# A gated linear attention and mixture-of-experts kernel on one core: one of two chunk masks done by ACT and GpSimd, row sums of two tiles at a time, keys split whole and placed by DMA

## The chip, the cores and the metric

The kernel runs on one core of a Trainium2 chip. The metric is the device time of one execution in microseconds, as the median of some runs. The core has five engines that each run their own instructions in order: PE (TensorE, matrix products, with weight loads shown apart as PEld), DVE (VectorE), ACT (ScalarE), POOL (GpSimd) and SP (SyncE, which here only issues DMAs). They wait for each other through semaphores. PE writes PSUM; POOL does not touch PSUM in this kernel.

## The reference

Two stages. The first is a gated linear attention over 4 batches, 8 heads, 768 positions and a head of 48; the second is a mixture of 4 attention experts on the first one's output, of which each position uses the best 2.

```python
for t in range(S):                                    # B, H, S, D = 4, 8, 768, 48
    state = alpha[:, :, t, :, None] * state + einsum('bhd,bhe->bhde', k[:, :, t], v[:, :, t])
    y[:, :, t] = einsum('bhd,bhde->bhe', q[:, :, t], state)
x = y.transpose(0, 2, 1, 3).reshape(B, S, H * D)      # 4 x 768 x 384
logits = x @ w_gate                                   # 4 experts, top 2, softmax over the two: w
for e in range(E):                                    # Hd = 64
    q, k, v = x @ wq[e], x @ wk[e], x @ wv[e]
    scores = where(causal, -1e9, scale * (q @ k.T))
    a = exp(scores - scores.max(-1)); a /= a.sum(-1) + 1e-09
    out += (weight of e at each position) * (a @ v @ wo[e])
```

## The kernel before

**First stage, by chunks.** The 768 positions of a batch are cut into 6 chunks of 128; there are 24 chunks, `n` = 0 to 23. For each, SP loads the gates (`al`), queries and keys side by side (`qk`) and values (`v`). `prep_r` (lines 172 to 182) makes the running products of the gates from the chunk's end with a DVE scan (L178) and multiplies the keys by them on POOL (L182). `prep_c` (184 to 190) makes those from its start (L188) and multiplies the queries (L190, DVE). `check` (L194, ACT) squares these products for a test of range at the end, in place; it can run only when both multiplications have read them. `gla_a` (196 to 208) forms the 128 x 128 products of keys and queries of 8 heads, `pa[0]` and `pa[1]`, four heads in each PSUM bank, and multiplies each bank by a causal 0/1 mask on DVE into `ms` (L207, one buffer). `gla_t` transposes the keys (`pt`, copied by ACT to `kt`), `gla_u` updates the state (`pu`; L241 on DVE, L242 on POOL), and `gla_y` multiplies `ms` and the state with values and queries into `py`, which is split into a rounded part `xh` (ACT, L268) and a remainder `xl` (DVE, L269).

**Second stage, by units.** Three chunks make a unit of 384 positions, `u` = 0 to 7; `hf` = u % 2 tells the first or second half of a batch. `front(u)` projects queries and keys of two pairs of experts (`proj`, PSUM `pj`, nine matrix products each), the values (`vproj`) and the gate's weights `gw` (`gate`). A projected tile is again split into a rounded part by ACT and a remainder by DVE. For queries this is done whole in `tq` (L405, L406), and four DMAs on SP's queue put the two halves of the partitions where the scores want them (L412). For keys, whose two experts lie in the two halves of the partitions, two ACT copies and two DVE subtractions write straight to `k0` and `k1` (L421 to L424).

`back(u)` goes through 12 tiles (pair, expert `e`, block `i` of 128 positions). `score` (471 to 510) multiplies queries and keys (`sc`; keys up to the diagonal: 128 to 384 columns in a first half, 512 to 768 in a second), takes the negative maximum on DVE (L491, L495), and lets ACT write exp to `a` (L498), whose running sum goes to `sm`. DVE then adds the one or two partial sums and 1e-9 (L503) and takes the reciprocal (L504); in units 1 to 7 POOL scales the row by it and by the gate's weight (L509), and in unit 0 DVE multiplies the two (L506) and ACT scales (L507). `AHEAD` = 4 scores later `transp` transposes `a` on PE (`tr`, L527) and ACT copies it to `at` (L538). When an expert pair is done, `av` multiplies with the values (`yv`), and at the unit's end `outp` forms `po`, `ot` and the output's DMA. `a` has `AB` = 7 buffers, `q` has `QB` = 6, and all PSUM tiles share 8 banks.

**What sets the order.** Up to the end of `rest` in the last lines of the program the instructions stand in the order of the code (`manual_schedule`). After that the streams are mixed by weights: `back(u)`, `front(u+1)` and `half(u+2)`, which is the first stage of the unit after next. A stream's account is raised by the cost of its matrix products and by `HOP` = 100 at each `yield`. The framework's scheduler then orders each engine's instructions by that sequence as priority and by its own estimate of when they are ready, so a small edit can move rows on every engine.

Of the kernel before, what the change touches and what calls it, by code (L numbers as in the profile page):

```python
# [54 lines left out]
def tile_gla_moe(ctx: ExitStack, tc: tile.TileContext, qk_d, al_d, v_d, wqk_d, wv_d, wo_d, nat_d, vn_d, out_d):  # L55
# [140 lines left out]
    def gla_a(n):  # L196
        t = gl["qk", n]
        ms = work.tile([128, 2, 4, C], F32, name="ms", bufs=1)
        gl["ms", n] = ms
        pa = [gp(f"pa{s}") for s in (0, 1)]  # L200
        for p in range(4):
            for s in (0, 1):
                r = 64 * s
                mm(pa[s][:, C * p:C * p + C], t[r:r + D, p, C:2 * C], t[r:r + D, p, 0:C],
                   110, start=True, stop=True, tile_position=(r, 0))
        for s in (0, 1):
            V.tensor_tensor(ms[:, s], pa[s].rearrange("p (a t) -> p a t", t=C),  # L207
                            mask[:, None, :].to_broadcast([128, 4, C]), OP.mult)
# [182 lines left out]
    def proj(u, pair, which):  # L391
        b, hf = divmod(u, 2)
        xh, xl = gl["x", u]
        col = 256 * which + 128 * pair
        cs = slice(col, col + 128)
        pj = gp("pj")
        i = 0
        for kt in range(3):
            for w, x in ((wqk_h, xh), (wqk_h, xl), (wqk_l, xh)):
                mm(pj[:, :W3], w[:, kt, cs], x[:, kt, :], W3 / 2.4, start=(i == 0), stop=(i == 8))  # L400
                i += 1
        if which == 0:
            mo["sm", u, pair] = SM[hf, pair]
            tq = work.tile([128, 2, W3], F32R, name="tq", bufs=1)
            A.activation(tq[:, 0], pj[:, :W3], AF.Copy)  # L405
            V.tensor_tensor(tq[:, 1], pj[:, :W3], tq[:, 0].bitcast(F32), OP.subtract)  # L406
            qs = []
            for e in (0, 1):
                q = work.tile([128, 2, W3], F32R, name="q", bufs=QB)
                src = tq[64 * e:64 * e + 64].bitcast(F32)  # L410
                for h in (0, 1):
                    SY.dma_start(q[64 * h:64 * h + 64].bitcast(F32), src)  # L412
                qs.append((q[:, 0], q[:, 1]))
            mo["q", u, pair] = qs
        else:
            if hf == 0:
# [4 lines left out]
            A.activation(k0[0:64, ts], pj[0:64, :W3], AF.Copy)  # L421
            A.activation(k1[64:128, ts], pj[64:128, :W3], AF.Copy)
            V.tensor_tensor(k0[64:128, ts], pj[0:64, :W3], k0[0:64, ts].bitcast(F32), OP.subtract)
            V.tensor_tensor(k1[0:64, ts], pj[64:128, :W3], k1[64:128, ts].bitcast(F32), OP.subtract)  # L424
# [46 lines left out]
    def score(u, pair, e, i):  # L471
        b, hf = divmod(u, 2)
        qh, ql = mo["q", u, pair][e]
        ks = mo["k", b, pair][e]
        sm = mo["sm", u, pair]
        ts = slice(128 * i, 128 * i + 128)
        n = 128 * (3 * hf + i + 1)
        c1 = 384 if n == 640 else min(n, 512)
# [16 lines left out]
            V.tensor_tensor(nm, mx[:, 0:1], mx[:, 1:2], OP.min)  # L495
        a = work.tile([128, S], F32, name="a", bufs=AB)
        for x, (c0, c1) in enumerate(pieces):
            A.activation(a[:, c0:c1], pss[x][:, :c1 - c0], AF.Exp, bias=nm, accum_out=sm[:, i, e, x:x + 1])  # L498
# [4 lines left out]
        V.tensor_scalar(den, den, 1e-9, sm[:, i, e, 1:2], op0=OP.add, op1=OP.add)  # L503
        V.reciprocal(cf, den)  # L504
        if u == 0:
            V.tensor_tensor(cf, cf, wt, OP.mult)  # L506
            A.activation(a[:, 0:n], a[:, 0:n], AF.Copy, scale=cf)  # L507
        else:
            G.tensor_scalar(a[:, 0:n], a[:, 0:n], cf, wt, op0=OP.mult, op1=OP.mult)  # L509
# [271 lines left out]
```

## Time and profile before

| | us |
|---|---|
| runs shown | 424.32, 419.24 and 1109.5; median 424.32 |
| profiled execution | 423.59, its span 421.9 |
| PE, DVE, ACT, POOL busy | 360.5, 289.0, 226.2, 123.3 |
| mean granted clock of PE | 0.939 |
| DVE in the masks (48) | 30.9 |
| DVE in sums and reciprocals of tiles (96 each) | 19.8 and 15.2 |
| DVE in the remainders of keys (32) | 8.9 and 8.8 |
| POOL in scaling (84) | 66.8 |

A row of the timeline gives start, duration, engine, line, operation, tiles, shapes, count, and in brackets the engine's idle time before it with what ended it. In a row of groups the count is followed by the busy time, the mean in ns, the idle time before, and who ended most of it. The granted clock is that of PE in a stretch, 1.00 being full speed. An engine that is idle costs something only where another one waits for it in the end.

### The profile page before, as it was taken

How to read it: one execution, taken by the hardware profiler on the slowest of the kernel's cores; microseconds unless marked ns; L12 is line 12 of the kernel's file. 1: busy time of each engine (PE TensorE's matmuls, PEld its weight loads, DVE VectorE, ACT ScalarE, POOL GpSimd, SP SyncE). 2: the span in 40 equal slices, each digit the busy share in tenths (PEclk: the TensorE clock that was granted, in tenths of full speed). 3: DMA queues.
4: the chain of work that ended last, by engine and by line, in shares of the span. 5: the costliest groups of instructions: out<-in, count | busy, mean ns of one | idle time of the engine just before them, and what ended most of it. 6: DMA issues, size and time to landing. Idle time of an engine off the chain costs nothing.

```text
span 421.9 us, 10017 instructions
## 1 busy us (share of the span) xinstructions
PE 360.5 (85%) x3758; PEld 294.6 (70%) x3758; DVE 289.0 (69%) x753; ACT 226.2 (54%) x637; POOL 123.3 (29%) x166
## 2 busy tenths in 40 slices
PE   6879676997797994998979869699999999999992
PEld 4659565886385773787848758378878877987772
DVE  5879799999589968177847777428737843578610
ACT  1254237576237745375344863636545766668941
POOL 3142331221214344025301723304402530134410
PEclk9899699699599998899989989799999999999998
DMA  8943596864371534063246223315134003420101
GB/s 231 331 127 89 138 272 175 230 161 122 111 196 51 158 109 123 15 189 93 89 121 197 82 80 113 75 58 151 47 96 111 2 2 77 131 64 13 57 20 47
DMA packets 20106, 48.03 MB, mean 114 GB/s; under 512 B 2704, under 2 KB 7120, under 8 KB 20048
## 3 DMA queue, kind: packets, MB, share of 16 engines
q1 hardware_dynamic: 16336, 42.11, 37.0%
q10 hardware_dynamic: 3712, 5.18, 3.5%
q8 instruction: 32, 0.52, 0.6%
q14 instruction: 26, 0.21, 0.2%
HBM read 29.98 MB, written 4.72 MB: 82 GB/s over the span
## 4 chain that ended last, share of the span: by engine, by line
PE 53%; DVE 19%; ACT 9%; DMA 8%; issue 6%; POOL 3%; SPq 1%; ACTq 0%; DVEq 0%; POOLq 0%
PE yv L72 11%; PE sc L72 7%; PE pj L72 7%; PE po L72 7%; PE py L72 6%; DMA qk<-in_qk_dram 5%; PE tr L527 5%; ACT a L498 4%; PE pv L72 3%; PE pa L72 3%; DVE mx L491 3%; DVE ms L207 2%; DVE al L188 2%; DVE al L178 2%; DVE qk L190 2%
## 5 line engine op out<-in xcount | busy, mean ns | idle before, releaser
L509 POOL TENSOR_SCALAR a<-a,sc,gw 128x512 f32<-128x512 f32 (+5 forms) x84 | 66.8, 800 | 165.4 <-DVE sc L504 69.9
L498 ACT ACTIVATE a<-sc,mx 128x256 f32<-128x256 f32 (+3 forms) x128 | 68.3, 542 | 25.2 <-DVE mx L495 11.1
L491 DVE TENSOR_REDUCE mx<-sc 128x1 f32<-128x256 f32 (+3 forms) x128 | 60.9, 499 | 20.6 <-PE sc L72 20.2
L527 PE MATMUL tr<-ident,a 128*128 128x128 f32 x336 | 55.4, 289 | 21.8 <-POOL a L509 12.2
L72 PE MATMUL sc<-k,q 128*128 128x384 f32 (+3 forms) x256 | 61.1, 348 | 4.1 <-ACT at L538 3.5
L527 PEld LDWEIGHTS tr<-ident,a 128*128 128x128 f32 x336 | 39.5, 147 | 26.9 <-POOL a L509 13.9
L538 ACT ACTIVATE at<-tr 128x512 f32<-128x512 f32 (+3 forms) x124 | 51.4, 462 | 6.7 <-PE tr L527 4.8
L72 PE MATMUL yv<-at,vg 128*64 128x384 f32 (+2 forms) x324 | 51.1, 414 | 3.6 <-ACT at L538 3.2
L182 POOL TENSOR_TENSOR qk<-qk,al 112x512 f32<-112x512 f32 (+1 forms) x26 | 31.8, 1227 | 71.3 <-DVE al L178 25.8
L72 PEld LDWEIGHTS sc<-k,q 128*128 128x128 f32 x256 | 42.1, 194 | 7.6 <-ACT at L538 3.8
L72 PE MATMUL pa<-qk 48*128 48x128 f32 x384 | 30.7, 298 | 16.0 <-issue 7.7
L72 PEld LDWEIGHTS yv<-at,vg 128*64 128x64 f32 x324 | 25.6, 143 | 24.5 <-issue 14.6
L72 PEld LDWEIGHTS pa<-qk 48*128 48x128 f32 x384 | 25.6, 198 | 19.0 <-issue 17.2
L72 PE MATMUL py<-ms,v 128*32 128x128 f32 x768 | 36.5, 283 | 2.7 <-ACT a L498 2.1
L72 PE MATMUL pj<-xh,wqk_h 128*128 128x384 f32 x96 | 36.7, 383 | 2.3 <-ACT xh L268 1.2
L188 DVE TENSOR_TENSOR_SCAN al<-al,d1c 112x516 f32<-112x516 f32 (+1 forms) x26 | 36.2, 1391 | 0.5
L194 ACT ACTIVATE al<-al 112x1032 f32<-112x1032 f32 x23 | 24.5, 1066 | 18.9 <-POOL qk L182 10.1
L72 PE MATMUL pj<-xl,wqk_h 128*128 128x384 f32 x96 | 33.8, 352 | 0.1
L72 PE MATMUL pj<-xh,wqk_l 128*128 128x384 f32 x96 | 33.6, 350 | 0.0
L178 DVE TENSOR_TENSOR_SCAN al<-al,d1r 112x516 f32<-112x516 f32 (+1 forms) x26 | 30.4, 1168 | 4.4 <-DMA al<-in_al_dram 4.1
L207 DVE TENSOR_TENSOR ms<-pa,mask 128x512 f32<-128x512 f32 x48 | 30.9, 686 | 3.3 <-PE pa L72 2.8
L503 DVE TENSOR_SCALAR sm<-sm 128x1 f32<-128x1 f32 x96 | 19.8, 208 | 18.2 <-ACT a L498 17.1
(100 smaller groups left out, 684.4 us busy)
## 6 DMA issues: line engine op xcount, KB each, us to landing
q<-tq SPq DMA_DIRECT2D x64, 192.0 KB, 3.4
al<-in_al_dram SPq DMA_DIRECT2D x21, 451.5 KB, 4.7
qk<-in_qk_dram SPq DMA_DIRECT2D x21, 448.0 KB, 5.2
v<-in_v_dram SPq DMA_DIRECT2D x24, 256.0 KB, 4.6
out_dram<-ot ACTq DMA_DIRECT2D x24, 192.0 KB, 1.9
al<-in_al_dram SPq DMA_DIRECT2D x6, 225.8 KB, 5.4
qk<-in_qk_dram SPq DMA_DIRECT2D x4, 224.0 KB, 6.2
wqk<-in_wqk_dram SPq DMA_DIRECT2D x1, 768.0 KB, 7.4
```

Source lines behind the costliest of these rows:

```text
L72: return PE.matmul(out, lhsT, rhs, **kw)
L178: V.tensor_tensor_scan(r.rearrange("p a w -> p (a w)"), r.rearrange("p a w -> p (a w)"), d1r[0:P, sl].rearrange("p a w -> p (a w)"), 0.0, ...
L182: G.tensor_tensor(t[0:P, sl, C:2 * C], t[0:P, sl, C:2 * C], r[:, :, 0:C], OP.mult)
L188: V.tensor_tensor_scan(c.rearrange("p a w -> p (a w)"), c.rearrange("p a w -> p (a w)"), d1[0:P, sl].rearrange("p a w -> p (a w)"), 0.0, O ...
L194: A.activation(al, al, AF.Square, accum_out=acc[0:P, n:n + 1])
L207: V.tensor_tensor(ms[:, s], pa[s].rearrange("p (a t) -> p a t", t=C), mask[:, None, :].to_broadcast([128, 4, C]), OP.mult)
L491: V.tensor_reduce(mx[:, x:x + 1], pp[:, :w], axis=AX.X, op=OP.max, negate=True)
L498: A.activation(a[:, c0:c1], pss[x][:, :c1 - c0], AF.Exp, bias=nm, accum_out=sm[:, i, e, x:x + 1])
L503: V.tensor_scalar(den, den, 1e-9, sm[:, i, e, 1:2], op0=OP.add, op1=OP.add)
L509: G.tensor_scalar(a[:, 0:n], a[:, 0:n], cf, wt, op0=OP.mult, op1=OP.mult)
L527: PE.transpose(pt[:, 128 * (j - j0):128 * (j - j0) + 128], a[:, 128 * j:128 * j + 128], ident)
L538: A.activation(dst, src, AF.Copy)
```

## The change

There are five edits.

- **Mask.** From chunk 3 on, the second bank `pa[1]` is copied to `ms` by ACT, and POOL sets to zero in place what lies beyond the diagonal (`affine_select` over 128 x 512). The first bank, and both banks of chunks 0 to 2, stay on DVE.
- **Row sums.** `score` ends with exp. A new step `norm` after every second score adds sums and 1e-9 for two tiles in one DVE operation with two inputs in SBUF, takes both reciprocals in one, and issues two POOL scalings. `sm` is laid out as one tile for each half of a batch.
- **Unit 0** is scaled on POOL as the others are.
- **Keys** of units 1 to 7 are split whole, as queries are, into `tk` (one buffer), and four DMAs of 64 partitions on SP's queue put the parts into `k0` and `k1`. Unit 0 keeps the old way.
- **Numbers.** `AHEAD` is 5 instead of 4; `q` has 5 buffers instead of 6.

```diff
-QB = 6
+QB = 5
-AHEAD = 4
+AHEAD = 5
...
         for s in (0, 1):
-            V.tensor_tensor(ms[:, s], pa[s].rearrange("p (a t) -> p a t", t=C),
-                            mask[:, None, :].to_broadcast([128, 4, C]), OP.mult)
+            src = pa[s].rearrange("p (a t) -> p a t", t=C)
+            if s == 0 or n < HALF:
+                V.tensor_tensor(ms[:, s], src, mask[:, None, :].to_broadcast([128, 4, C]), OP.mult)
+            else:
+                A.activation(ms[:, s], src, AF.Copy)
+                G.affine_select(ms[:, s], ms[:, s], [[0, 4], [1, C]], OP.is_ge, 0.0, base=-(C - 1),
+                                channel_multiplier=1)
...
-            A.activation(k0[0:64, ts], pj[0:64, :W3], AF.Copy)
-            A.activation(k1[64:128, ts], pj[64:128, :W3], AF.Copy)
-            V.tensor_tensor(k0[64:128, ts], pj[0:64, :W3], k0[0:64, ts].bitcast(F32), OP.subtract)
-            V.tensor_tensor(k1[0:64, ts], pj[64:128, :W3], k1[64:128, ts].bitcast(F32), OP.subtract)
+            if u == 0:
...
+            else:
+                tk = work.tile([128, 2, W3], F32R, name="tk", bufs=1)
+                A.activation(tk[:, 0], pj[:, :W3], AF.Copy)
+                V.tensor_tensor(tk[:, 1], pj[:, :W3], tk[:, 0].bitcast(F32), OP.subtract)
+                for e, k in enumerate((k0, k1)):
+                    for h in (0, 1):
+                        SY.dma_start(k[64 * h:64 * h + 64, ts].bitcast(F32), tk[64 * e:64 * e + 64, h].bitcast(F32))
...
-            A.activation(a[:, c0:c1], pss[x][:, :c1 - c0], AF.Exp, bias=nm, accum_out=sm[:, i, e, x:x + 1])
-        eg = 2 * pair + e
-        wt = mo["w", u][:, i, eg:eg + 1]
-        den = sm[:, i, e, 0:1]
-        cf = work.tile([128, 1], F32, name="sc", bufs=4)
-        V.tensor_scalar(den, den, 1e-9, sm[:, i, e, 1:2], op0=OP.add, op1=OP.add)
-        V.reciprocal(cf, den)
-        if u == 0:
-            V.tensor_tensor(cf, cf, wt, OP.mult)
-            A.activation(a[:, 0:n], a[:, 0:n], AF.Copy, scale=cf)
-        else:
-            G.tensor_scalar(a[:, 0:n], a[:, 0:n], cf, wt, op0=OP.mult, op1=OP.mult)
+            A.activation(a[:, c0:c1], pss[x][:, :c1 - c0], AF.Exp, bias=nm, accum_out=sm[:, x:x + 1])
         mo["a", u, pair, e, i] = a
+
+    def norm(u, *tiles):
+        hf = u % 2
+        ix = [6 * pair + 3 * e + i for pair, e, i in tiles]
+        sm = SM[hf][:, ix[0]:ix[1] + 1:ix[1] - ix[0]]
+        cf = work.tile([128, 2], F32, name="sc", bufs=4)
+        V.scalar_tensor_tensor(cf, sm[:, :, 0], 1e-9, sm[:, :, 1], op0=OP.add, op1=OP.add)
+        V.reciprocal(cf, cf)
+        for x, (pair, e, i) in enumerate(tiles):
+            a = mo["a", u, pair, e, i]
+            n = 128 * (3 * hf + i + 1)
+            eg = 2 * pair + e
+            G.tensor_scalar(a[:, 0:n], a[:, 0:n], cf[:, x:x + 1], mo["w", u][:, i, eg:eg + 1], op0=OP.mult, op1=OP.mult)
...
                 score(u, *seq[k])
                 yield
+                if k % 2:
+                    norm(u, seq[k - 1], seq[k])
+                    yield
```

What this does to the order of the engines is shown at three places. The line numbers of the changed kernel differ: its masks are L209 (DVE), L211 (ACT) and L212 (POOL), its maxima L503, its sums L518 and L519, its scaling L524, its transposes L541.

On DVE, in unit 0, about where the second to fifth tiles are summed; `sm` holds partial sums, `sc` here the reciprocals. Before:

```order
L491 TENSOR_REDUCE mx<-sc 128x1
L504 RECIPROCAL sc<-sm_113 128x1
L178 SCALAR_TENSOR_TENSOR al<-al,d1r 112x516
L506 TENSOR_TENSOR sc<-sc,gw 128x1
L503 TENSOR_SCALAR sm_113<-sm_113 128x1 x2
L504 RECIPROCAL sc<-sm_113 128x1
L503 TENSOR_SCALAR sm_113<-sm_113 128x1
L506 TENSOR_TENSOR sc<-sc,gw 128x1
L504 RECIPROCAL sc<-sm_113 128x1 x2
L180 RECIPROCAL d1c_82<-al 112x4
L506 TENSOR_TENSOR sc<-sc,gw 128x1 x2
L188 SCALAR_TENSOR_TENSOR al<-al,d1c_82 112x516
```

In the changed kernel:

```order
L503 TENSOR_REDUCE mx<-sc 128x1 x3
L518 SCALAR_TENSOR_TENSOR sc<-sm_113 128x2
L180 RECIPROCAL d1c_82<-al 112x4
L503 TENSOR_REDUCE mx<-sc 128x1
L519 RECIPROCAL sc<-sc 128x2
L188 SCALAR_TENSOR_TENSOR al<-al,d1c_82 112x516
L518 SCALAR_TENSOR_TENSOR sc<-sm_113 128x2
L190 TENSOR_TENSOR qk<-qk,al 112x4x128
```

The eleven small operations ahead of the scan L188 have become one sum and one reciprocal of two tiles; the second pair's sum stands behind the scan.

On PE, at the end of unit 1. Before, this is the end of chunk 11's `py`, with the values of pair 0 (`yv`) in its midst:

```order
L72 MATMUL sc<-cmaskb,identb 128x128
L72 MATMUL yv<-at,vg 64x384
L72 MATMUL py<-ms,v 32x128 x4
L72 MATMUL py<-qk,S_94 32x128 x4
L72 MATMUL py<-ms,v 32x128 x4
L72 MATMUL py<-qk,S_94 32x128
L72 MATMUL yv<-at,vg 64x384 x7
L72 MATMUL yv<-at,vg 64x256 x2
L72 MATMUL yv<-at,vg 64x128 x2
L72 MATMUL py<-qk,S_94 32x128 x3
```

In the changed kernel the same `yv` follows the unit's last score, and the query projection of unit 2's second pair follows it; 24 transposes come after that projection:

```order
L72 MATMUL sc<-k_759,q 128x512 x2
L72 MATMUL sc<-k_759,q 128x256 x2
L72 LDWEIGHTS identb
L72 MATMUL sc<-cmaskb,identb 128x128
L72 MATMUL yv<-at,vg 64x384 x8
L72 MATMUL yv<-at,vg 64x256 x2
L72 MATMUL yv<-at,vg 64x128 x2
L72 MATMUL pj<-xh,wqk_h 128x384
```

So these twelve instructions of `yv` moved from within chunk 11's `py` to behind the last score.

On POOL, from chunk 5's preparation to unit 0's first tiles (`S` is the state). Before:

```order
L182 TENSOR_TENSOR qk<-qk,al 112x4x128 x2
L242 TENSOR_TENSOR S_94<-st,ev 48x4x48 x2
L182 TENSOR_TENSOR qk<-qk,al 112x4x128 x3
L242 TENSOR_TENSOR S_92<-st,ev 48x4x48 x2
L182 TENSOR_TENSOR qk<-qk,al 112x4x128 x2
```

In the changed kernel:

```order
L182 TENSOR_TENSOR qk<-qk,al 112x4x128 x2
L247 TENSOR_TENSOR S_94<-st,ev 48x4x48 x2
L212 AFFINE_SELECT ms<-ms 128x512 x2
L182 TENSOR_TENSOR qk<-qk,al 112x4x128
L524 TENSOR_SCALAR a<-a,sc,gw 128x128
L524 TENSOR_SCALAR a<-a,sc,gw 128x256
L524 TENSOR_SCALAR a<-a,sc,gw 128x384
L524 TENSOR_SCALAR a<-a,sc,gw 128x128
L182 TENSOR_TENSOR qk<-qk,al 112x4x128
L212 AFFINE_SELECT ms<-ms 128x512
```

The selects of chunks 5 and 6 stand ahead of the multiplication of a later chunk's keys, and unit 0's scalings stand between such multiplications.

More of the change, by code (lines that the diff above doesn't have):

```diff
@@ L128, in tile_gla_moe @@
     acc = consts.tile([128, NG], F32)
-    SM = {}
+    SM = []
     for hf in (0, 1):
-        for pair in (0, 1):
-            SM[hf, pair] = consts.tile([128, 3, 2, 2], F32, name=f"sm{hf}{pair}")
-            G.memset(SM[hf, pair], 0.0)
+        t = consts.tile([128, 2 * NE * 3, 2], F32, name=f"sm{hf}")
+        G.memset(t, 0.0)
+        SM.append(t)
     wraw = {}
@@ L402, in proj @@
         if which == 0:
-            mo["sm", u, pair] = SM[hf, pair]
             tq = work.tile([128, 2, W3], F32R, name="tq", bufs=1)
@@ L420, in proj @@
             ts = slice(W3 * hf, W3 * hf + W3)
-            A.activation(k0[0:64, ts], pj[0:64, :W3], AF.Copy)
-            A.activation(k1[64:128, ts], pj[64:128, :W3], AF.Copy)
-            V.tensor_tensor(k0[64:128, ts], pj[0:64, :W3], k0[0:64, ts].bitcast(F32), OP.subtract)
-            V.tensor_tensor(k1[0:64, ts], pj[64:128, :W3], k1[64:128, ts].bitcast(F32), OP.subtract)
+            if u == 0:
+                A.activation(k0[0:64, ts], pj[0:64, :W3], AF.Copy)
+                A.activation(k1[64:128, ts], pj[64:128, :W3], AF.Copy)
+                V.tensor_tensor(k0[64:128, ts], pj[0:64, :W3], k0[0:64, ts].bitcast(F32), OP.subtract)
+                V.tensor_tensor(k1[0:64, ts], pj[64:128, :W3], k1[64:128, ts].bitcast(F32), OP.subtract)
+            else:
[5 more added lines that the diff above has]
+                        SY.dma_start(k[64 * h:64 * h + 64, ts].bitcast(F32), tk[64 * e:64 * e + 64, h].bitcast(F32))
     def vproj(u, i):
@@ L474, in score @@
         ks = mo["k", b, pair][e]
-        sm = mo["sm", u, pair]
+        sm = SM[hf][:, 6 * pair + 3 * e + i]
         ts = slice(128 * i, 128 * i + 128)
```

## Prediction

> **What bounds the kernel now.** I read the page's totals first, then the busy time by stage, then TensorE's (PE's) idle gaps in the timeline, and last the other engines around one such gap.
>
> ```profile
> span 421.9 us, 10017 instructions
> PE 360.5 (85%) x3758; PEld 294.6 (70%) x3758; DVE 289.0 (69%) x753; ACT 226.2 (54%) x637; POOL 123.3 (29%) x166
> PE 53%; DVE 19%; ACT 9%; DMA 8%; issue 6%; POOL 3%; SPq 1%; ACTq 0%; DVEq 0%; POOLq 0%
> ```
>
> PE is the engine with most to do, and it holds about half of the chain that ended last. The change takes nothing off PE, so what it can win lies in the 61 us in which PE is idle (421.9 less 360.5). The stages differ (span, then PE, PEld, DVE, ACT and POOL busy, then PE's granted clock):
>
> ```profile
> 0.00:40.00 40.00, 31.82 (x383) 25.47 (x383) 30.20 (x48) 14.53 (x31) 12.29 (x33) 0.96 0.67 192
> 40.00:110.00 70.00, 52.44 (x662) 44.45 (x661) 65.06 (x149) 36.84 (x103) 16.62 (x18) 0.86 0.73 190
> 110.00:300.00 190.00, 165.60 (x1694) 133.32 (x1694) 127.84 (x330) 101.67 (x291) 62.08 (x71) 0.93 0.37 107
> 300.00:400.00 100.00, 97.23 (x910) 81.11 (x908) 63.23 (x220) 66.47 (x198) 30.12 (x43) 1.00 0.23 61
> ```
>
> From 40 to 110 VectorE (DVE) is busy 65.06 of 70 us and PE has 17.6 us idle: there DVE sets the pace. From 110 to 300 DVE is busy two thirds of the time and PE still loses 24 us. After 300 PE loses 2.8 us in 100 and nothing is to be had. The first 40 us hold no edited instruction that PE waits for. So the gaps between 40 and 300 are what counts; these are the large ones (start, duration, idle time before in brackets and what ended it):
>
> ```profile
> 46.34 2.08 PE L72 MATMUL pa<-qk 48*128 48x128 f32 x16 [3.84 <-issue]
> 57.95 1.16 PE L72 MATMUL pa<-qk 48*128 48x128 f32 x16 [3.07 <-DVE qk L190]
> 74.35 1.02 PE L72 MATMUL pa<-qk 48*128 48x128 f32 x6 [4.02 <-DVE S L239]
> 104.98 0.69 PE L527 MATMUL tr<-ident,a 128*128 128x128 f32 x2 [1.51 <-DVE k L424]
> 109.67 1.54 PE L72 MATMUL yv<-at,vg 128*64 128x384 f32 x2 [1.81 <-ACT at L538]
> 163.30 0.63 PE L527 MATMUL tr<-ident,a 128*128 128x128 f32 x4 [2.69 <-ACT at L538]
> 167.78 1.54 PE L527 MATMUL tr<-ident,a 128*128 128x128 f32 x6 [3.16 <-POOL a L509]
> 213.78 0.47 PE L527 MATMUL tr<-ident,a 128*128 128x128 f32 x1 [3.06 <-POOL a L509]
> 248.26 1.22 PE L72 MATMUL sc<-k,q 128*128 128x512 f32 x2 [3.51 <-ACT at L538]
> 266.79 0.74 PE L527 MATMUL tr<-ident,a 128*128 128x128 f32 x5 [1.31 <-ACT at L538]
> 270.15 1.54 PE L527 MATMUL tr<-ident,a 128*128 128x128 f32 x6 [2.62 <-POOL a L509]
> ```
>
> They sum to 30.6 us and are of two kinds: chunk preparation late on DVE (the three before pa, 10.9 us), and the end of a unit's tiles, when the transposes `tr` have caught up with scaling (the rest). How a unit's end comes about, at unit 1:
>
> ```profile
> 153.68 1.70 SPq L88 DMA_DIRECT2D qk<-in_qk_dram  x2
> 159.08 0.69 DVE L190 TENSOR_TENSOR qk<-qk,al 112x512 f32<-112x512 f32 x1 [1.97 <-DMA qk<-in_qk_dram]
> 159.20 2.76 POOL L182 TENSOR_TENSOR qk<-qk,al 112x512 f32<-112x512 f32 x2 [6.00 <-DMA qk<-in_qk_dram]
> 160.85 1.06 ACT L194 ACTIVATE al<-al 112x1032 f32<-112x1032 f32 x1 [3.64 <-POOL qk L182]
> 165.73 2.00 POOL L509 TENSOR_SCALAR a<-a,sc,gw 128x768 f32<-128x768 f32 x1 [3.78 <-ACT at L538]
> ```
>
> A load goes out only when a chunk's last reader is done (153.68) and is used at 159.08. DVE, POOL and then ACT sit in order behind it, the last tile is scaled only from 165.73, and PE runs out of other work meanwhile.
>
> **The change part by part.** The prices (count, then busy us and mean ns of one):
>
> ```profile
> L503 DVE TENSOR_SCALAR sm<-sm 128x1 f32<-128x1 f32 x96 | 19.8, 208 | 18.2 <-ACT a L498 17.1
> L504 DVE RECIPROCAL sc<-sm 128x1 f32<-128x1 f32 x96 | 15.2, 159 | 4.3
> L506 DVE TENSOR_TENSOR sc<-sc,gw 128x1 f32<-128x1 f32 x12 | 3.7, 319 | 0.1
> L207 DVE TENSOR_TENSOR ms<-pa,mask 128x512 f32<-128x512 f32 x48 | 30.9, 686 | 3.3 <-PE pa L72 2.8
> L424 DVE TENSOR_TENSOR k<-pj,k 64x384 fp32r<-64x384 f32 x16 | 8.9, 559 | 0.3
> L538 ACT ACTIVATE at<-tr 128x512 f32<-128x512 f32 x48 | 28.6, 605 | 4.7 <-PE tr L527 3.0 <-PE yv L72 1.2
> L509 POOL TENSOR_SCALAR a<-a,sc,gw 128x512 f32<-128x512 f32 x16 | 13.6, 851 | 34.2 <-ACT tq L405 29.9 <-DVE sc L504 3.1 <-ACT at L538 1.1
> L116 POOL TENSOR_SCALAR_AFFINE_SELECT mask<-mask 128x128 f32<-128x128 f32 x1 | 0.3, 293 | 0.0
> L507 ACT ACTIVATE a<-a,sc 128x128 f32<-128x128 f32 (+2 forms) x12 | 5.9, 505 | 6.0 <-DVE sc L506 3.3 <-DVE gw L454 1.2 <-DVE d1c L180 1.1
> ```
>
> Masks: for chunks 3 to 23 one of two DVE multiplications goes, 21 x 0.686 = 14.4 us. In its place stand an ACT copy of the same size out of PSUM (0.605 by the `at` copy, 12.7 us in all) and a POOL select of 128x512, which the trace does not show. Its bounds are 0.293 (the select of a quarter of the columns) and 4 x 0.293 = 1.17; I take 0.9, next to the 0.851 of POOL's one-input pass over the same size: 19 us more on POOL. py follows pa closely only at chunks 3 to 5 (one pj or pv and little else between); a copy and a select, 1.5 us, take the place of the 1.3 us of two masks there, and I charge 1 us for POOL's queue. While the select waits for its copy, the next multiply of keys by their products and the next tile's scaling wait behind it on POOL, and PE's transposes for the latter; on ACT a `kt` copy stands behind the new copy. At a unit's end, where that would hurt, the order has other work on PE (below).
>
> Row sums: 96 x (0.208 + 0.159) + 12 x 0.319 = 39 us leave DVE; 48 pairs of a two-input sum and a reciprocal come. A two-input operation on such a sliver is L506, 0.319; with 0.159 that is 48 x 0.478 = 23 us, or 18 us at the price of L503; I take 18 here and charge the rest below, as a cost, so DVE's net is -21. The wait for exp now is for two tiles at once, and what stands behind it on DVE (maxima, scans) waits with it; before, DVE waited 17.1 us on these sums, so I charge nothing more, and at worst 0.2 x 48 = 10 us.
>
> Keys: in units 1 to 7, 14 DVE operations of 0.559 (7.8 us) and 14 ACT copies go. 56 DMAs come, on SP's queue behind the queries':
>
> ```profile
> 164.27 2.40 SPq L412 DMA_DIRECT2D q<-tq  x4
> q<-tq SPq DMA_DIRECT2D x64, 192.0 KB, 3.4
> ```
>
> That is 0.6 us an issue and 3.4 us to landing. A key is projected during the preceding unit's tiles, over 10 us of PE work ahead of its first score, so I take 0; without that cover a unit's start waits 2.4 + 3.4 = 5.8 us. The loads behind them on SP can be 2.4 us later a pair, but most stand waiting for a py anyway. One q buffer fewer makes SP wait for three scores of the running unit; same answer.
>
> Unit 0: 12 ACT passes of 0.505 become POOL passes of at most 0.851. DVE in all: -14.4 - 21 - 7.8 = -43 us; ACT about even; POOL +19 + 8.
>
> Now the gaps, place by place. Preparation (10.9 us): up to 74 us DVE loses four masks (2.7) and the sums of five tiles (3.4), and gets about 1.2 back; the first gap is another matter, as its scan is blocked:
>
> ```profile
> 41.60 3.91 DVE L188 TENSOR_TENSOR_SCAN al<-al,d1c 112x516 f32<-112x516 f32 x1
> 42.62 1.80 POOL L170 TENSOR_TENSOR wo_l<-wo,wo_h 128x768 fp32r<-128x768 f32 x1
> ```
>
> The scan ends 1.1 us after POOL's pass does, at 45.51. I take -4 of 10.9. Unit 0's end (3.3): the other seven tiles' sums and ACT's passes go, -2. Unit 1's end (5.85): five tiles instead of four are outstanding, and the order puts the whole `yv` of pair 0 between the last score and the first of these transposes. Such a `yv`, and a projection with and without a gap before it, take in the chain:
>
> ```profile
> 169.32 2.88 PE pj L72 x9
> 172.21 3.61 PE yv L72 x24
> 179.44 1.63 PE pj L72 x9
> ```
>
> So 3.4 to 3.6 us of work that ran before the wait now runs inside it: -5 of 5.85. Unit 2's end has the shorter `yv`: -2.5 of 3.06. The gap at 248 is ACT and DVE behind a load, and its order is unchanged: -0.5. Unit 3's end (3.93) is like unit 1's: -3. Sum -17. The projection after the gap at 167 took 2.88 instead of 1.63: 1.25 us more go with each gap that closes, -4 for three or four.
>
> Costs: the new two-input sums and the scans meet more POOL work, and L506 took 0.160 more than the one-input L504 beside it: 48 x 0.160 = 7.7 us of DVE, a third of it on the path, +3; masks +1; in the tail two scalings instead of one follow the last exp, +1. So -17 - 4 + 5 = -16 on the profiled execution, which took 423.6 (1.7 around its span; the median of the runs shown is 424.3): **408 us**, and by the bounds of the places 400 to 416.
>
> The Trainium skill, SBUF — State Buffer, section "Who interferes with whom", says that a DVE operation with two SBUF inputs and a POOL operation that reads SBUF exclude each other for the whole instruction. The scan of 3.91 us over POOL's passes agrees. It speaks against this change, which adds both kinds; taken to its end it is the second rival.
>
> **Rivals.** First, the loads bind. Rows 153.68 to 159.20 show every engine behind a transfer that the change does not start sooner. Then only preparation and unit 0's end gain, 6 us, less about 2: 419. Against it: the load's 5.4 us did not change, but PE gets 3.5 us more to do meanwhile.
>
> Second, DVE and POOL exclude each other. From 40 to 110 POOL gets 6 selects and 12 scalings, 6 x 0.9 + 12 x 0.6 = 12.6 us; if all of it holds up scans and sums there, it eats what DVE is freed of: the 6 us of those stages fall away, and I put 2 more on the unit ends: 416. For it: the scan at 41.60. Against it: POOL is busy 16.62 of 70 there, and few scans of that stage are as long.
>
> Third, slower: POOL becomes the last engine at every unit's end. If the last pair is scaled later than PE has `yv` and projection for (5.2 us after the last score), PE waits for a select (0.9) and a second scaling (0.851) more at each of 8 ends, +14; four lost clocks, +5; preparation's -4 stands: 423.6 + 15 = 438. For it: the POOL wait in three of the gaps above, and a buffer of `a` less to spare. Against it: POOL is at 29% of the span.
>
> Fourth, better: all gaps but that at 248 close, -27, with -5 for the clock and the same +5: 397.
>
> **How the numbers follow.** Forecast 0.55, loads 0.18, exclusion 0.10, slower 0.11, better 0.06. The range is 396 to 426, which leaves out the slower case and some ends, under 2 in 10; the forecast's own is 400 to 416. A measurement of this kernel can tell about 2% from no change, so below 415.8 is faster and above 432.8 slower: of the forecast nearly all (0.53), of exclusion and loads little (0.04), and the better case give 0.63 faster; the third rival mostly gives 0.11 slower; 0.26 is left for within 2%.
>
> **What would show it.** Right: DVE busy near 250 us (289 less 43, plus what exclusion gives back), POOL near 150, PE's waits for POOL's `a` at unit 1, 2 and 3's ends under 1 us, and 40 to 110 with PE idle under 13 us in the same work. The first step to fail would be the select: a mean over 1.2 us, or py waiting for it. The pair's sum at a mean over 0.35 shows exclusion. Gaps of 3 us before `tr` with DVE behind L190 show that loads bind. If PE waits for POOL's `a` more than 12 us in all, the third rival holds. The prediction is wrong if PE's idle time stays within 5 us of 61, or falls by over 30.

## The result, and the profile after

| | before | changed |
|---|---|---|
| median of the runs, us | 422.70 | 402.14 |
| ratio, 95% interval | | 0.953 [0.945, 0.961] |
| profiled execution, its span, us | 423.59, 421.9 | 407.95, 406.1 |
| PE busy, PE idle, us | 360.5, 61.4 | 358.7, 47.4 |
| mean granted clock of PE | 0.939 | 0.945 |

The change is faster, by 20.6 us in the medians. The profiled execution of the changed kernel was a disturbed one, some 6 us longer and at a lower clock (0.945) than its other runs (0.952 to 0.958), so its gaps can be read by place, but its span, its PE busy time and its total of idle time compare only roughly with those of the other kernels. The page's totals, as shown of before, are now:

```profile
span 406.1 us, 9981 instructions
PE 358.7 (88%) x3758; PEld 297.7 (73%) x3758; DVE 258.1 (64%) x610; ACT 224.0 (55%) x632; POOL 154.1 (38%) x197
```

DVE lost 31 us of work and POOL got 31. By stage (span, then PE, PEld, DVE, ACT and POOL busy, then PE's granted clock; unit 0 ends near 104 now, near 110 before):

```profile
40.00:104.00 64.00, 50.48 (x702) 43.53 (x701) 57.54 (x116) 33.11 (x92) 37.85 (x37) 0.93 0.81 208
104.00:290.00 186.00, 169.02 (x1763) 139.06 (x1767) 119.43 (x286) 106.84 (x309) 72.19 (x86) 0.94 0.48 130
290.00:384.00 94.00, 93.95 (x848) 79.79 (x842) 50.21 (x159) 64.35 (x192) 30.73 (x44) 1.00 0.34 86
```

In the first stretch PE idles 13.5 us (17.6 before), in the second 17.0 us, where from 110 to 300 it was 24.4. The gaps of PE in its timeline, at the places of the prediction's list and near them (idle time in brackets, and what ended it):

```profile
48.43 1.16 PE L72 MATMUL pa<-qk 48*128 48x128 f32 x16 [2.18 <-POOL wo_l L170]
57.99 2.08 PE L72 MATMUL pa<-qk 48*128 48x128 f32 x16 [4.12 <-DVE qk L190]
73.12 1.16 PE L72 MATMUL pa<-qk 48*128 48x128 f32 x16 [1.11 <-DVE sc L519]
99.43 0.52 PE L541 MATMUL tr<-ident,a 128*128 128x128 f32 x3 [1.35 <-DVE tk L433]
102.50 0.45 PE L541 MATMUL tr<-ident,a 128*128 128x128 f32 x1 [2.55 <-DVE st L246]
104.36 1.31 PE L541 MATMUL tr<-ident,a 128*128 128x128 f32 x5 [1.42 <-DVE xl L274]
159.82 0.74 PE L541 MATMUL tr<-ident,a 128*128 128x128 f32 x5 [0.89 <-DVE yl L573]
201.06 0.44 PE L541 MATMUL tr<-ident,a 128*128 128x128 f32 x2 [0.94 <-POOL a L524]
202.42 0.52 PE L541 MATMUL tr<-ident,a 128*128 128x128 f32 x3 [0.93 <-DVE yl L573]
208.68 0.62 PE L72 MATMUL po<-wo_h,yl 128*128 128x384 f32 x2 [1.61 <-DVE yl L573]
224.22 0.66 PE L541 MATMUL tr<-ident,a 128*128 128x128 f32 x4 [2.21 <-POOL a L524]
237.88 0.73 PE L72 MATMUL sc<-k,q 128*128 128x512 f32 x2 [2.14 <-ACT at L552]
256.21 2.15 PE L541 MATMUL tr<-ident,a 128*128 128x128 f32 x15 [0.50 <-DVE yl L573]
```

The first three are the preparation, 7.4 us in place of 10.9. The next three are unit 0's end, which is no better. Unit 1's end (159.82) and unit 3's (256.21) have all but closed; unit 2's end (201.06 to 208.68) has not, and the gap before 224.22 is new, as is one of 1.78 us at 141.74 (not among these lines), where `pv` waits for ACT's exp. PE's waits for POOL's `a`, 12.2 us in 8 waits before, are down to this row of the waits by line (us in all, times, longest):

```profile
PE tr L541 <- POOL a L524: 4.2, 3, 2.2
```

### The profile page after: what moved, and what is told of

Same layout as the page of the kernel before. It is cut to its first block, busy times and chain, and to the rows that moved or that the text cites. A ratio compares the mean times of both kernels' runs of the same rounds, so it can differ in the third digit from the quotient of the medians.

```text
span 406.1 us, 9981 instructions
## 1 busy us (share of the span) xinstructions
PE 358.7 (88%) x3758; PEld 297.7 (73%) x3758; DVE 258.1 (64%) x610; ACT 224.0 (55%) x632; POOL 154.1 (38%) x197
## 4 chain that ended last, share of the span: by engine, by line
PE 50%; DVE 20%; DMA 10%; ACT 10%; issue 5%; POOL 2%; SPq 1%; ACTq 0%; DVEq 0%; POOLq 0%
PE yv L72 8%; PE pj L72 8%; PE sc L72 7%; PE po L72 7%; PE tr L541 6%; DMA al<-in_al_dram 5%; PE py L72 5%; DMA qk<-in_qk_dram 5%; DVE al L178 5%; DVE al L188 3%; PE pv L72 3%; PE pa L72 3%; ACT al L194 2%; ACT a L510 2%; DVE mx L503 2%
## 5 line engine op out<-in xcount | busy, mean ns | idle before, releaser
L524 POOL TENSOR_SCALAR a<-a,sc,gw 128x128 f32<-128x128 f32 (+5 forms) x96 | 75.7, 798 | 83.7 <-DVE sc L519 49.9
L503 DVE TENSOR_REDUCE mx<-sc 128x1 f32<-128x256 f32 (+3 forms) x128 | 60.8, 498 | 25.9 <-PE sc L72 25.3
L541 PE MATMUL tr<-ident,a 128*128 128x128 f32 x336 | 53.6, 289 | 12.8 <-POOL a L524 4.2
L541 PEld LDWEIGHTS tr<-ident,a 128*128 128x128 f32 x336 | 39.9, 148 | 17.1 <-POOL a L524 7.4
L72 PE MATMUL yv<-at,vg 128*64 128x384 f32 (+2 forms) x324 | 49.7, 404 | 2.6 <-ACT at L552 2.6
L182 POOL TENSOR_TENSOR qk<-qk,al 112x512 f32<-112x512 f32 (+1 forms) x26 | 35.5, 1366 | 38.8 <-DVE al L178 26.3
L72 PEld LDWEIGHTS sc<-k,q 128*128 128x128 f32 x256 | 43.0, 197 | 7.0 <-ACT at L552 2.4
L72 PEld LDWEIGHTS yv<-at,vg 128*64 128x64 f32 x324 | 27.1, 139 | 22.0 <-issue 9.3
L247 POOL TENSOR_TENSOR S<-st,ev 48x192 f32<-48x192 f32 x32 | 18.1, 567 | 60.3 <-DVE st L246 59.5
L194 ACT ACTIVATE al<-al 112x1032 f32<-112x1032 f32 x23 | 24.4, 1062 | 22.3 <-DVE mx L507 7.0
L212 POOL TENSOR_SCALAR_AFFINE_SELECT ms<-ms 128x512 f32<-128x512 f32 x21 | 18.4, 875 | 46.2 <-ACT ms L211 45.5
L188 DVE TENSOR_TENSOR_SCAN al<-al,d1c 112x516 f32<-112x516 f32 (+1 forms) x26 | 33.7, 1295 | 0.5
```

Of the source, the lines that this page charges most:

```text
L72: return PE.matmul(out, lhsT, rhs, **kw)
L182: G.tensor_tensor(t[0:P, sl, C:2 * C], t[0:P, sl, C:2 * C], r[:, :, 0:C], OP.mult)
L188: V.tensor_tensor_scan(c.rearrange("p a w -> p (a w)"), c.rearrange("p a w -> p (a w)"), d1[0:P, sl].rearrange("p a w -> p (a w)"), 0.0, O ...
L194: A.activation(al, al, AF.Square, accum_out=acc[0:P, n:n + 1])
L212: G.affine_select(ms[:, s], ms[:, s], [[0, 4], [1, C]], OP.is_ge, 0.0, base=-(C - 1), channel_multiplier=1)
L247: G.tensor_tensor(Ln[rows, :, cols], st[rows], e, OP.mult)
```

## The experiments

Twelve kernels were run with three rounds each. Medians and ratios are against the kernel before on the same chip (421.96 to 423.3 us there).

| kernel | us | ratio, 95% interval |
|---|---|---|
| the changed kernel with four scores ahead (`e1_ahead4`) | 429.43 | 1.017 [1.009, 1.025] |
| before with five ahead (`e2_only_ahead5`) | 401.05 | 0.948 [0.942, 0.954] |
| before with six ahead (`e7_only_ahead6`) | 410.21 | 0.969 [0.965, 0.973] |
| the same with eight buffers for `a` (`e12_ahead6_ab8`) | 409.80 | 0.970 [0.960, 0.980] |
| changed, sums of single tiles (`e5_sums_single`) | 394.95 | 0.934 [0.930, 0.938] |
| the same with four ahead (`e9_single_ahead4`) | 420.88 | 0.997 [0.993, 1.001] |
| e5 with an empty step after every second score (`e14_single_yield`) | 400.47 | 0.945 [0.937, 0.953] |
| changed, both masks on DVE (`e3_masks_dve`) | 405.28 | 0.959 [0.953, 0.966] |
| e5 with both masks on DVE (`e10_single_masks_dve`) | 400.17 | 0.947 [0.939, 0.955] |
| changed, keys the old way (`e4_keys_old`) | 410.23 | 0.969 [0.962, 0.975] |
| e5 with keys the old way (`e15_single_keys_old`) | 404.36 | 0.957 [0.949, 0.964] |
| before with five ahead and keys by DMA (`e8_ahead5_keys`) | 400.13 | 0.943 [0.936, 0.949] |

The theory put to the test was that the unit ends close because five scores run ahead (cover), not because DVE has less to do (relief); the rival was the relief.

### How many scores run ahead

`e1_ahead4` takes the fifth score back out of the changed kernel, `e2_only_ahead5` puts it alone into the kernel before.

```diff
 # e1_ahead4, in the changed kernel
-AHEAD = 5
+AHEAD = 4
 # e2_only_ahead5, in the kernel before
-AHEAD = 4
+AHEAD = 5
```

> The changed kernel with the transposes four scores behind instead of five; nothing else differs. Theory of cover: most of the gain comes at the unit ends, from the values of pair 0 standing behind the last score; with four that product runs before one or two scores again, so half or more of the 20 us is lost: 410 to 414. Theory of relief: the gain is the 31 us that DVE has less to do, wherever it falls; then this kernel stays at 401 to 405.

> The kernel before with the transposes five scores behind; nothing else differs. Theory of cover: the unit ends' gaps shrink without any relief of DVE, 410 to 414. Theory of relief: DVE, ACT and POOL have the same work in the same queues, so 419 to 424, no difference.

The one line gives 21 us in the kernel before, as much as the whole change. Without it, the other edits together are 7.5 us slower than before, though DVE then has the least to do of all three:

```profile
span 425.8 us, 9966 instructions
PE 360.9 (85%) x3758; PEld 299.4 (70%) x3758; DVE 253.8 (60%) x610; ACT 227.1 (53%) x632; POOL 152.5 (36%) x197
PE tr L541 <- POOL a L524: 27.2, 11, 5.2
```

That is `e1_ahead4`: DVE 253.8 us, and 27.2 us of PE's idle time wait for scaled tiles. `e2_only_ahead5` has the opposite:

```profile
span 400.2 us, 10030 instructions
PE 353.7 (88%) x3758; PEld 290.8 (73%) x3758; DVE 287.7 (72%) x753; ACT 224.9 (56%) x637; POOL 124.2 (31%) x166
```

DVE has its 287.7 us as before, and no wait for POOL's `a` is left among PE's longest twelve by line. Of its 21.7 us of span against before, 14.9 are idle time of PE (61.4 to 46.5) and 6.8 are PE's busy time for the same 3758 products, at a granted clock of 0.959 in place of 0.939. So the fifth score makes the gain, and relief without it makes none. Both times lie outside the 410 to 414 that was written down for cover: the effect is about twice what was thought.

That it works by cover can be seen at unit 1's end. The 26 transposes of the last five tiles follow the last score (its mask product is the row of `cmaskb`) after 9.8 us of other work on PE in `e2_only_ahead5`, the `yv` of pair 0 among it, and run without a gap:

```profile
149.76 0.23 PE L72 MATMUL sc<-cmaskb,identb 128*128 128x128 bf16 x1
154.32 3.45 PE L72 MATMUL yv<-at,vg 128*64 128x384 f32 x24
159.77 3.00 PE L527 MATMUL tr<-ident,a 128*128 128x128 f32 x26
```

In the kernel before, the last score ends at 157.35, these transposes begin 1.5 us later, and the rest of them comes after the gaps of 2.69 and 3.16 us (and one of 0.37) that the prediction lists at 163.30 and 167.78:

```profile
158.82 1.80 PE L527 MATMUL tr<-ident,a 128*128 128x128 f32 x15
```

At the ends of units 1 to 3 and at the gap at 248 together, 16.4 us of gaps become 3.9 us (0.96, 0.65, 1.10 and 1.23), which is 12.4 of the 14.9. At unit 1's end `e1_ahead4` shows how a pair makes the missing cover worse (ACT's exp, DVE's sum and reciprocal, POOL's scaling, PE's transposes):

```profile
147.67 0.64 ACT L510 ACTIVATE a<-sc,mx 128x384 f32<-128x384 f32 x1
148.23 0.55 ACT L510 ACTIVATE a<-sc,mx 128x256 f32<-128x256 f32 x1
...
161.72 0.47 ACT L510 ACTIVATE a<-sc,mx 128x256 f32<-128x256 f32 x1
...
162.36 0.14 DVE L518 SCALAR_TENSOR_TENSOR sc<-sm 128x2 f32<-128x2 f32 x1
162.53 0.17 DVE L519 RECIPROCAL sc<-sc 128x2 f32<-128x2 f32 x1
162.80 1.84 POOL L524 TENSOR_SCALAR a<-a,sc,gw 128x640 f32<-128x640 f32 x2 [6.80 <-DVE sc L519]
163.73 0.77 PE L541 MATMUL tr<-ident,a 128*128 128x128 f32 x5 [4.31 <-POOL a L524]
```

The tile of 640 columns (384 and 256) has its exp by 148.9, but its partner, the unit's last tile, only at 162.2. Both are scaled from 162.80, and PE, which wants the first of them, has idled 4.31 us.

Is still more better? `e7_only_ahead6` sets six in the kernel before, `e12_ahead6_ab8` also gives `a` an eighth buffer.

```diff
 # e12_ahead6_ab8, in the kernel before; e7_only_ahead6 has the last change alone
-AB = 7
+AB = 8
-QB = 6
+QB = 5
-AHEAD = 4
+AHEAD = 6
```

> The kernel before with the transposes six scores behind. With five it took 401 and PE no longer waited for POOL's scaling, so the theory of cover expects nothing more: 399 to 403. If more distance always helps: 390 to 396. If the seven buffers of the scaled rows now bind (seven are in use at once): 404 to 412.

> The kernel before with six scores ahead of the transposes in place of four, and with eight buffers for the weights a in place of seven (five for the queries in place of six, which makes the room). Nothing of the computation is left out. Six ahead with seven buffers took 410.21 us where five took 401.05. Theory A: six outstanding tiles leave one buffer of seven, so exp waits for the transposes of the oldest tile: with eight buffers the time falls back to 399 to 402 us. Theory B: it is the end of the unit, where six tiles' transposes and their ACT copies come in one run and the copies bind: the time stays at 408 to 412 us, and PE's waits for ACT's copies stay near 9 us.

Six is 9 us worse than five, and the eighth buffer gives none of it back, so the buffers are not the reason. PE's waits for ACT's copies are this row in both kernels:

```profile
PE yv L72 <- ACT at L538: 9.1, 9, 2.1
```

With five it is 5.1 us in 6 waits. Of the 6.9 us between the profiled spans of six and five (407.1 and 400.2), 4.2 are idle time of PE (50.7 and 46.5), as much as these waits have grown, and 2.7 are its busy time, at a clock of 0.956 instead of 0.959. Why the copies come later with six was not followed. No gap of PE above 2.7 us stands between 110 and 290 in either.

### Two tiles at a time

`e5_sums_single` gives the changed kernel the old sum, reciprocal and scaling of each tile, directly after its exp; `e9_single_ahead4` is that with four ahead.

```diff
+        cf = work.tile([128, 1], F32, name="sc", bufs=4)
+        V.tensor_scalar(sm[:, 0:1], sm[:, 0:1], 1e-9, sm[:, 1:2], op0=OP.add, op1=OP.add)
+        V.reciprocal(cf, sm[:, 0:1])
+        eg = 2 * pair + e
+        G.tensor_scalar(a[:, 0:n], a[:, 0:n], cf, mo["w", u][:, i, eg:eg + 1], op0=OP.mult, op1=OP.mult)
...
-                if k % 2:
-                    norm(u, seq[k - 1], seq[k])
-                    yield
```

> The changed kernel with sum, reciprocal and scaling of each tile at once after its score, as in the kernel before; masks, keys, five scores and unit 0 on POOL stay. If pairing is a relief of DVE only and the fifth score hides its wait: 404 to 408, as DVE gets about 16 us back. If the pair's wait still costs at unit ends: 396 to 401.

> The same with the transposes four scores behind. With pairs and four it was 429. If it is pairing that makes four scores too few (the first of two tiles waits for the second's exp, and the second for the first's scaling): 412 to 421, no slower than the kernel before. If it is the selects in POOL's queue: 426 to 432, and pairing is innocent.

At both distances single tiles are faster, 402.14 to 394.95 with five and 429.43 to 420.88 with four. `e9_single_ahead4` is also the plainest trial of relief: mask, keys and unit 0 take 23 us off DVE (265.6 us busy, 289.0 before), and with four scores ahead the time is that of the kernel before (0.997 [0.993, 1.001]). `e5_sums_single`, below both of the ranges written down for it, beats the kernel before and the changed one, and its page shows that DVE's busy time was no guide:

```profile
span 392.7 us, 10158 instructions
PE 351.9 (90%) x3758; PEld 291.1 (74%) x3758; DVE 270.2 (69%) x706; ACT 222.9 (57%) x632; POOL 152.7 (39%) x197
```

DVE is busy 12 us longer than in the changed kernel, and PE idles 40.8 us instead of 47.4. `e14_single_yield` asks whether the pair's wait or its extra `yield` (which raises the second stage's account by `HOP`) costs the 7 us.

```diff
 # in e5_sums_single
                 score(u, *seq[k])
                 yield
+                if k % 2:
+                    yield
```

> This is the changed kernel with sums, reciprocals and scalings of single tiles (394.95 us in an earlier run, against 402.14 with pairs), to which one empty step is added after every second score: the mixing of the streams counts a hop there, as it does after the changed kernel's pair step, and nothing is issued in it. Nothing of the computation is left out. Theory A: pairing costs by its wait, since the first of two tiles is scaled only after the second one's exp, so that its transposes find it late: then the empty step costs nothing, 393 to 397 us. Theory B: pairing costs by the extra hop, which moves the second stage against the first in the mixed order: then the time goes back to 400 to 404 us. Between 397 and 400 both have a part.

The empty step alone brings the time to 400.47 (runs from 398.8 to 402.0; e5's were 394.4 to 396.8). So with five ahead most of the cost, 5.5 of 7.2 us (4.5 of 7.9 by the ratios), comes with another hop, though nothing is issued in it. In the two profiled executions 3.0 us of it are idle time of PE (40.8 and 43.8) and 4.5 its busy time (351.9 and 356.4), at a clock of 0.963 and 0.956. Some 2 to 3 us are left for what else a pair brings, the wait of the first tile and a sum with two inputs, which POOL can hold up (the last section). The times tell neither these apart nor the whole from none, but the traces show longer waits for scaled tiles: PE waits 4.2 us for POOL's `a` in the changed kernel, 0.6 in `e5_sums_single` and 0.2 in `e14_single_yield`. With four ahead the two were not separated; there the wait is to be seen in the trace above.

### Masks, keys and unit 0

```diff
 # e3_masks_dve in the changed kernel, e10_single_masks_dve in e5
-            if s == 0 or n < HALF:
+            if True:
 # e4_keys_old in the changed kernel, e15_single_keys_old in e5
-            if u == 0:
+            if True:
```

`e8_ahead5_keys` is the kernel before with `AHEAD` = 5, `QB` = 5 and the keys by DMA as in the change's diff.

> The changed kernel with both masks on DVE, as before: DVE gets 14 us back, POOL loses 18 us of selects, ACT 12 us of copies. Theory of cover: the masks matter only up to 75 us, 402 to 406. Theory of relief: 14 of the 31 us are undone, so 9 us of the 20 are lost, 409 to 413. A third theory, that POOL's selects hold up scans and sums as much as they free DVE: 400 to 402, or faster than the change.

> The best version so far (the changed kernel with single-tile sums, 394.95 us) with both chunk masks on DVE, as in the kernel before. Nothing of the computation is left out. DVE gets back 21 masks of 0.686 us, 14 us; POOL loses 21 selects, 18 us. Theory A (cover, not DVE's load, decides): PE waits for neither, 393 to 397 us, and with less work on POOL ahead of the scalings perhaps a little better. Theory B (DVE's relief is worth something once scaling is in time): from 40 to 100 us PE idles some 4 us more and the time is 399 to 404 us.

> The changed kernel with the keys written by two ACT copies and two DVE subtractions in all units, and no DMAs for them: DVE gets 7.8 us back, ACT 6.8, SP loses 56 DMAs. Theory of cover: 401 to 404. Theory of relief: a quarter of DVE's relief is undone, 405 to 408. Were the DMAs themselves in the way of loads, this kernel would be faster than the change by 2 to 4 us.

> The best version so far (the changed kernel with single-tile sums, 394.95 us) with the keys of all units written by two ACT copies and two DVE subtractions, as in the kernel before; the queries keep five buffers. Nothing of the computation is left out. Undoing the keys cost 8 us in the changed kernel with its pairs, and adding them to the kernel before with a fifth score ahead gave 1 us. Theory A (the 8 us come from what the order makes of the pairs): 394 to 398 us. Theory B (the keys' own relief of DVE and ACT): 400 to 404 us.

> The kernel before with five scores, keys split whole and placed by DMA, and five q buffers; masks, sums and unit 0 as before. Taking the DMA keys out of the changed kernel cost 8 us. If that is the keys' own worth, this kernel is as much below the 401 of five scores alone: 392 to 396. If it was the order that fell badly there: 399 to 403.

`e8_ahead5_keys` and `e10_single_masks_dve` differ in unit 0's scaling (ACT or POOL) and in how `sm` is laid out: 400.13 and 400.17, so these are worth nothing that shows. The rest, at five ahead with sums of single tiles (us):

| | both masks on DVE | one mask by ACT and POOL |
|---|---|---|
| keys the old way | 401.05 (`e2_only_ahead5`) | 404.36 (`e15_single_keys_old`) |
| keys by DMA | 400.17 (`e10_single_masks_dve`) | 394.95 (`e5_sums_single`) |

`e2_only_ahead5` differs from the other three also in unit 0's scaling by ACT, in the layout of `sm` and in having six `q` buffers; the buffers were not tried by themselves. Neither edit gains by itself: the keys alone 1 us, which the runs hardly tell from none, the mask alone loses 3; both together gain 6. It is PE's idle time that shows this, 46.5 and 49.1 us in the upper row and 46.3 and 40.8 in the lower one. Part of it has a place. The mask's move shortens the preparation, in PE's timeline of `e10_single_masks_dve` and then of `e5_sums_single`:

```profile
46.50 2.08 PE L72 MATMUL pa<-qk 48*128 48x128 f32 x16 [3.83 <-issue]
57.95 1.37 PE L72 MATMUL pa<-qk 48*128 48x128 f32 x16 [3.51 <-DVE qk L190]
74.36 0.90 PE L72 MATMUL pa<-qk 48*128 48x128 f32 x11 [3.34 <-DVE sm L513]
```

```profile
46.77 1.16 PE L72 MATMUL pa<-qk 48*128 48x128 f32 x16 [2.18 <-POOL wo_l L170]
56.34 2.08 PE L72 MATMUL pa<-qk 48*128 48x128 f32 x16 [4.13 <-DVE qk L190]
72.35 1.16 PE L72 MATMUL pa<-qk 48*128 48x128 f32 x16 [1.44 <-POOL a L516]
```

10.7 us become 7.8. `e15_single_keys_old` has the short form too (7.6 us) and is slower all the same; at unit 0's end it has four gaps of over 1 us (6.6 us), of which the largest is this one, in a place where `e5_sums_single` has none:

```profile
108.33 1.54 PE L72 MATMUL yv<-at,vg 128*64 128x384 f32 x2 [2.77 <-ACT at L557]
```

The mask's copies add to ACT what the keys by DMA take off it (ACT is busy 228.8 us in `e15_single_keys_old`, 222.9 in e5, 224.9 in `e2_only_ahead5`), which would fit the table, but `e10_single_masks_dve`, with ACT at 212.8, waits as long there. What makes the two edits need each other is not settled: each one also reorders every engine.

With pairs, undoing the masks costs 3 us (`e3_masks_dve`) and undoing the keys 8 (`e4_keys_old`), a time above all three theories for the latter. The profiled spans of these two, 403.0 and 409.6, do not differ in idle time: PE idles 46.7 us in both, and is busy 356.3 and 362.9 us for the same products, at a clock of 0.954 and 0.942. So no wait shows that these 8 us are the keys' relief.

## Why the prediction was right

The forecast was 408 us in a range of 396 to 426, 16 us less than before; 20.6 were measured. The mechanism, cover at the unit ends, was right. The terms of its sum, put against what the runs show:

| step of the prediction | forecast | shown |
|---|---|---|
| the fifth score: unit 1 to 3's ends, the gap at 248, the clock | -15 | -21 (`e2_only_ahead5`) |
| relief: preparation, unit 0's end | -6 | -6 for mask, keys and unit 0 together (`e5_sums_single` against `e2_only_ahead5`); by place, 2.8 in the preparation and 2.2 at unit 0's end |
| costs: lock, masks' queue, tail | +5 | +7 (`e5_sums_single` to the changed kernel, which differ in the pairs alone) |

That the last row comes near is luck: it was charged to lock, queue and tail, and most of what was paid came with the pairs' extra step in the order, which the sum had at nothing; at most the 2 to 3 us beside it can be the lock. The first row, which holds the whole gain, was 6 us too small.

**Unit ends.** Right in place and size where the longer `yv` came in: at unit 1's end 5.85 us became 0.89, at unit 3's 3.93 became 0.50 and a wait of 0.67 for `yv`. At unit 2's end the step failed: 3.06 us became two gaps of 0.9 before `tr` and one of 1.6 before `po`. Single tiles leave less there, 0.96 and 0.65 in `e2_only_ahead5`, 0.80 and 1.26 in `e5_sums_single`; the wait for POOL's `a` is in neither.

**The clock.** This is the term that was mis-sized. I took 4 us from one projection before and after a gap; `e2_only_ahead5` has PE busy 6.8 us less for the same products (the changed kernel's profiled execution only 1.8). Together with 14.9 us less idle time that is 21.7 where the sum had 15.

**Preparation.** -4 forecast, 10.9 to 7.4 measured, and the mask is the cause (10.7 and 7.8 above, with sums of single tiles). PE idled 13.5 us from 40 to unit 0's end, where the sign of being right was under 13. The blocked first scan is now at L190, which ends behind the same POOL pass over `wo`.

**Unit 0's end.** -2 forecast, nothing gained: 5.3 us in the three gaps above, for 5.4 in four before. In `e5_sums_single` it is 3.5, so pairing took it.

**Prices.** DVE lost 31 us instead of 43. The masks, sums and keys went about as forecast:

```profile
L212 POOL TENSOR_SCALAR_AFFINE_SELECT ms<-ms 128x512 f32<-128x512 f32 x21 | 18.4, 875 | 46.2 <-ACT ms L211 45.5
L211 ACT ACTIVATE ms<-pa 128x512 f32<-128x512 f32 x21 | 12.4, 589 | 10.1 <-PE pa L72 6.6 <-POOL S L247 3.4
L518 DVE SCALAR_TENSOR_TENSOR sc<-sm 128x2 f32<-128x2 f32 x48 | 11.3, 236 | 17.9 <-ACT a L510 16.3 <-ACT gw L468 1.3
L519 DVE RECIPROCAL sc<-sc 128x2 f32<-128x2 f32 x48 | 7.7, 159 | 0.9
L507 DVE TENSOR_TENSOR mx<-mx 128x1 f32<-128x1 f32 x32 | 11.0, 344 | 0.2
k<-tk SPq DMA_DIRECT2D x56, 96.0 KB, 2.8
```

The select took 0.875 us in the mean (0.9 assumed; 0.635 where nothing holds it up, so the hit is in part luck), the pair's sum 0.236 (under the 0.35 that was to show exclusion), the keys' DMAs land after 2.8 us and the only wait of PE for them in these runs is one of 1.3 us, in `e1_ahead4`. The sums and reciprocals came to 19 us, 20 less than before. What I did not have is in L507, the minimum of two maxima, at 344 ns where it was 240 (L495): it too has two inputs in SBUF and now meets more POOL work. That is 3.3 us, and the gate's small operations take 2 more; the remainder is spread.

**The pairs' wait** was costed at nothing, at worst 10 us. The larger part lay elsewhere: at five ahead an extra step costs 4.5 to 5.5 us by itself, and some 2 to 3 are left for the wait and the two-input sum. The order rows were read for three places, and the account of the mixing was not among them.

**The rivals.** Loads binding (419) falls: the load's wait is still there and unit 1's end closed. Exclusion (416) has the lock right (the last section) and its price wrong: POOL was busy 37.85 us from 40 to unit 0's end, 16.62 before, and the preparation gained 3.5 us all the same. The better case (397) wanted 27 us of gaps closed; PE's idle time fell by 14. POOL last at every end (438) falls as a whole, 4.2 us of waits for `a`; the change without the fifth score comes near it (429.43, 27.2 us). Its milder form is the new gap at 222. Two tiles had their reciprocal at 220.75, but ahead of their scaling POOL's order has a multiplication of a chunk's keys, and POOL stood before it for 3.19 us; DVE's L190 beside it waited for a load:

```profile
220.60 0.15 DVE L519 RECIPROCAL sc<-sc 128x2 f32<-128x2 f32 x1
...
221.68 0.69 DVE L190 TENSOR_TENSOR qk<-qk,al 112x512 f32<-112x512 f32 x1 [0.93 <-DMA qk<-in_qk_dram]
221.80 1.61 POOL L182 TENSOR_TENSOR qk<-qk,al 112x512 f32<-112x512 f32 x1 [3.19 <-PE sc L72]
222.29 1.87 DVE L507 TENSOR_TENSOR mx<-mx 128x1 f32<-128x1 f32 x1
223.40 1.62 POOL L524 TENSOR_SCALAR a<-a,sc,gw 128x512 f32<-128x512 f32 x2
```

## What to carry to other kernels

Where an engine idles at the end of a batch of tiles and the work that could fill the time stands just ahead of it in its own order, one more tile in flight moves that work into the gap; here it was worth 21 us by itself, while one more again lost 9. Taking work off a busy engine is worth only what some wait for it was: with four tiles ahead, 23 us less of DVE's time changed nothing, and 35 us less, by pairs, went with a time 7.5 us longer. A step that batches small operations is also a step in the schedule, so run it once empty before its price is put down to the batching.

## What the runs showed of the hardware

**A sliver on DVE can wait for a whole pass on POOL.** The sum of the pair at 155.89 has two columns and takes 1.16 us, until POOL's multiplication is over; the one at 220.20 took 0.15:

```profile
155.42 1.62 POOL L182 TENSOR_TENSOR qk<-qk,al 112x512 f32<-112x512 f32 x1 [1.73 <-DMA qk<-in_qk_dram]
155.89 1.16 DVE L518 SCALAR_TENSOR_TENSOR sc<-sm 128x2 f32<-128x2 f32 x1
```

At 222.29, quoted above, L507 sits out the rest of POOL's multiplication and the first of the two scalings behind it, 1.87 us for one column. The same sum with one SBUF input and a scalar column (`e5_sums_single`) stays between 0.181 and 0.216 us in all its 96 executions. The Trainium skill, SBUF — State Buffer, section "Who interferes with whom", says this: a DVE instruction with two SBUF inputs and a POOL instruction that reads SBUF exclude each other, by a lock on a shared pair of ports, and one with at most one such input does not contend, outside the two-port modes. These rows agree.

**It goes both ways.** The select takes 0.635 us when nothing holds it up (the median of its 21) and 1.49 behind a scan of DVE that began 0.16 us earlier:

```profile
42.31 1.22 DVE L178 TENSOR_TENSOR_SCAN al<-al,d1r 112x516 f32<-112x516 f32 x1
42.47 1.49 POOL L212 TENSOR_SCALAR_AFFINE_SELECT ms<-ms 128x512 f32<-128x512 f32 x1 [0.20 <-ACT ms L211]
```

Its rest after the scan's end at 43.53 is 0.43 us, less than its whole 0.635. The same is seen on DVE: the L190 of 0.69 us that begins at 45.08 ends 0.55 us after POOL's pass over `wo`.

**PE's busy time goes with its granted clock, and the clock only in part with PE's idle time.** For the same 3758 products PE is busy 360.5 us at a mean clock of 0.939 (the kernel before), 353.7 at 0.959 (`e2_only_ahead5`), 351.9 at 0.963 (`e5_sums_single`) and 349.7 at 0.966 (`e8_ahead5_keys`). In the first three the idle time falls as the clock rises (61.4, 46.5, 40.8 us). But `e10_single_masks_dve`, `e2_only_ahead5`, `e3_masks_dve` and `e4_keys_old` all idle between 46.3 and 46.7 us, at clocks of 0.961, 0.959, 0.954 and 0.942, and their spans go from 396.8 to 409.6. So the clock is not a function of the idle time alone, and a difference of some us between two of these kernels can be the clock with no wait behind it; what else sets the clock stays open.
